# Polysketch attention and cosine router on one core: a reordered start of the early experts, key sums taken earlier, a routing maximum and a row write cut in two

## The chip, the cores and the metric

One Trainium2 chip, one core of it. The metric is the device time of one execution in microseconds (us), lower is better. The kernel before was run three times: 200.28, 197.08 and 200.38 us, a median of 200.28 us.

## The reference, cut to what matters

The first half is attention with a product feature map, without a softmax. `S1` and `S2` are 8 x 32, heads have 32 columns, so each key and query becomes 64 features. The second half takes the four heads' outputs as 128-column tokens, sends each of the 4352 tokens to one of eight experts by a cosine, and applies that expert's two-layer MLP.

```python
def phi(x):
    a = np.einsum('rd,bhsd->bhsr', S1, x)
    b = np.einsum('rd,bhsd->bhsr', S2, x)
    return np.einsum('bhsi,bhsj->bhsij', a, b).reshape(*x.shape[:-1], r * r)
q_p, k_p = phi(q), phi(k)                        # batch 4, heads 4, seq 1088
kv = np.einsum('bhsf,bhsd->bhfd', k_p, v)
z = np.sum(k_p, axis=2)
num = np.einsum('bhsf,bhfd->bhsd', q_p, kv)
den = np.einsum('bhsf,bhf->bhs', q_p, z)[..., None] + 1e-06
x = (num / den).transpose(0, 2, 1, 3).reshape(B * S, H * D)
...
logits = xn @ en.T / tau                         # xn, en: rows of x and expert_emb, normalised
expert_idx = np.argmax(logits, axis=1)
gate_w = softmax(logits)[token, expert_idx]
for e in range(E):                               # w1[e]: 128 x 1024, w2[e]: 1024 x 128
    h = np.maximum(x[mask] @ w1[e], 0.0)
    out[mask] = gate_w[mask, None] * (h @ w2[e])
```

## The kernel before, in words

**Stages.** Two batches are worked together as a half, m = 0 and m = 1; a half has 17 tiles of 128 tokens, held as 4 + 4 + 4 + 4 tiles and one rest tile ("r"). For each group of four, keys and queries are turned by TensorE (`ktr`, `qtr`), multiplied by the sketches (`kab`, `qab`, or `pairs` for the queries of half 0), and the two factors are multiplied into features (`kp`, `qp`, `prod`). The keys' features times the values are summed into one PSUM bank (`kv`), together with the factors' own sums; `total` copies that bank, `kve` turns it by head with two kinds of matmuls (`by_head`, and `ones_e` for the denominators) and `kz` copies the result. The queries' features, turned (`trqp`, `qpT`), times that matrix give attention outputs and expert logits at once (`nd`, 32 recorded matmul passes of about 1.3 us for a group), and VectorE divides (`x`, lines 672 to 684).

**Routing.** For half 0, once all four `x 0 ...` are there, `best` takes the maximum of each token's eight logits and subtracts it (lines 733 to 735), `pick` makes the one-hot choice, `write` sends the rows (128 columns of output and 8 logits) to HBM by `rows<-xg`, and a chain of VectorE and TensorE steps (`place 0`, `count`, `take`, `split`, `mark`, `find`, `sums`, `tokens`) gives the token numbers of the first blocks, `dst_i`, and the experts of these blocks. GpSimd then gathers rows (`fetch`, line 1043, tile `xs`), SyncE's queue loads the expert's first layer (`weights`, tile `wb`, 512 KB), and TensorE runs the blocks.

**The blocks.** 35 blocks of 128 tokens. Block i is `turn(i)` (one transpose), `up(i)` (16 recorded passes `ps_big<-xTb,wb`), a Relu on ScalarE (`hT`, line 1108), and `down(i)` (16 passes on `w_sb,hT` into the banks acc or ab). `down` chooses its expert at run time, so it needs all sixteen pieces of the second layers (`w_sb`, 256 KB each) on the chip.

**What sets the order.** The order on every engine is written by hand: `HEAD` and `ORDER` (lines 395 to 410) are lists of step names that are executed as they stand, `AFTER_TURN` adds the steps that stand behind `turn 1`. So half 1's `nd 1 0` and `nd 1 1` stand in front of `up(0)`, `nd 1 2` and `nd 1 3` between `turn 1` and `up(1)`. The step `ld` issues the next piece of half 1's values and queries and then of the second layers; each waits for the last TensorE instruction in front of it, and all loads, the row writes and the first layers share SyncE's one queue. `nd` and `up` take turns on the two double banks `ps_big`: `up(0)` reuses the bank of `nd 1 0` (free when `x 1 0` has read it), `nd 1 2` reuses that of `nd 1 1` (free when `x 1 1` has read it).

## Time and profile before

| | us |
|---|---|
| median of three runs (lowest, highest) | 200.28 (197.08, 200.38) |
| profiled execution, its own time | 199.14 |
| its span, first to last instruction | 197.2 |
| outside the span | 1.94 |
| TensorE matmuls busy in the span | 188.3 (95%) |
| TensorE weight loads busy | 177.8 (90%) |
| VectorE, ScalarE, GpSimd busy | 87.9, 99.1, 107.6 |
| granted TensorE clock | 1.00 throughout |

In the timeline a row is: start in us, duration, engine, line, operation, the tile written and the tiles read, shapes, count; the square bracket tells how long the engine had been idle before it and what ended that. A count of x16 on matmuls counts recorded passes; a 32-bit product of one pair of tiles shows as two. PEld is TensorE's loading of weights, which runs beside its matmuls. In a windows row stand the stretch, its length, the busy time of each engine, the granted clock, the share of the DMA engines' time and GB/s.

### The profile page before, as it was taken

The numbers are of one execution on the slowest core, as the hardware profiler recorded it, in microseconds if no ns is written. First come the engines' busy times: TensorE is split into PE (matmuls) and PEld (weight loads), VectorE is DVE, ScalarE is ACT, GpSimd is POOL, SyncE is SP. The second block draws the span as 40 slices with busy tenths as digits, with TensorE's granted clock in tenths as the row PEclk, the third lists the DMA queues.
The fourth block names the chain that finished last, engine by engine and source line by source line (L and its number), as shares of the span: only waits on it lengthen the run. The fifth ranks groups of instructions, "written<-read, shape, count | busy, mean of one in ns | idle before, by whom it ended". The sixth has DMA issues, their size and how long they took to land.

```text
span 197.2 us, 7104 instructions
## 1 busy us (share of the span) xinstructions
PE 188.3 (95%) x2667; PEld 177.8 (90%) x2667; DVE 87.9 (45%) x393; ACT 99.1 (50%) x280; POOL 107.6 (55%) x135
## 2 busy tenths in 40 slices
PE   7999899999979999999999999999999999999990
PEld 7677799788869999999999999999999999998890
DVE  6589868798378489922221221221221221222100
ACT  2675542437253456433564654654654654766430
POOL 4300054707713866565977767767767767733052
PEclk9999999999999999999999999999999999999999
DMA  5979968974799997544587686596665655540001
GB/s 139 345 203 276 237 172 221 331 232 124 201 281 330 285 338 209 188 136 149 149 263 237 158 288 201 155 281 211 161 195 182 160 200 180 150 137 12 3 20 32
DMA packets 29924, 38.32 MB, mean 194 GB/s; under 512 B 5721, under 2 KB 23394, under 8 KB 29890
## 3 DMA queue, kind: packets, MB, share of 16 engines
q1 hardware_dynamic: 27600, 33.18, 56.3%
q0 software_dynamic: 2240, 4.67, 7.6%
q8 instruction: 23, 0.38, 0.8%
q14 instruction: 11, 0.09, 0.2%
q10 hardware_dynamic: 50, 0.01, 0.0%
HBM read 33.25 MB, written 4.66 MB: 192 GB/s over the span
## 4 chain that ended last, share of the span: by engine, by line
PE 75%; DMA 12%; DVE 6%; issue 2%; ACT 2%; POOLq 1%; POOL 0%
PE ps_big L155 35%; PE ps_acc L155 14%; PE ps_ab L155 14%; DMA xs<-rows,dst_i 12%; PE ps_t L158 6%; PE ps_t L155 3%; PE ps_acc L111 1%; DVE xg L679 1%; DVE row L779 1%; PE ps_ab L158 1%; PE ps_acc L158 1%; POOLq L1300 1%; DVE qp L458 1%; PE ps_big L158 1%; ACT hT L1108 1%
## 5 line engine op out<-in xcount | busy, mean ns | idle before, releaser
L155 PE MATMUL ps_big<-xTb,wb 128*128 128x128 f32 (+2 forms) x608 | 70.6, 266 | 0.1
L155 PEld LDWEIGHTS ps_big<-xTb,wb 128*128 128x128 f32 (+1 forms) x608 | 66.7, 183 | 1.5 <-issue 0.9
L1149 POOL DMA_INDIRECT out_dram<-y,dst_i x35 | 36.4, 1041 | 42.3 <-ACT sq L1113 21.4
L1108 ACT ACTIVATE hT<-ps_big 128x1024 f32<-128x1024 f32 x35 | 35.8, 1023 | 41.3 <-issue 23.6
L1043 POOL DMA_INDIRECT xs<-rows,dst_i x35 | 36.7, 1048 | 13.0 <-issue 6.1
L155 PE MATMUL ps_acc<-w_sb,hT 128*128 (+2 forms) x288 | 35.1, 275 | 0.0
L1051 DVE COPY xTb<-ps_t 128x128 f32<-128x128 f32 x28 | 8.1, 291 | 57.3 <-issue 39.7
L155 PEld LDWEIGHTS ps_acc<-w_sb,hT 128*128 128x128 f32 (+2 forms) x288 | 33.3, 184 | 0.3 <-issue 0.2
L155 PE MATMUL ps_ab<-w_sb,hT 128*128 (+1 forms) x272 | 33.2, 275 | 0.0
L155 PEld LDWEIGHTS ps_ab<-w_sb,hT 128*128 128x128 f32 (+1 forms) x272 | 31.6, 187 | 0.1
L1114 POOL TENSOR_TENSOR norm<-norm,half_c 128x1 f32<-128x1 f32 x35 | 20.7, 595 | 5.2 <-ACT sq L1113 4.9
L1127 DVE TENSOR_SCALAR gate<-gate 128x1 f32<-128x1 f32 x35 | 5.3, 150 | 21.2 <-ACT probs L1124 19.7
L458 POOL TENSOR_TENSOR kp<-both 128x1024 f32<-128x1024 f32 (+1 forms) x4 | 7.2, 1812 | 12.5 <-ACT both L499 11.1
L155 PE MATMUL ps_big<-kz,held 128*64 128x82 f32 x256 | 10.7, 236 | 1.1 <-ACT xTb L1051 1.1
L1146 ACT ACTIVATE y<-ps_ab,gate 128x128 f32<-128x128 f32 x17 | 6.2, 367 | 10.9 <-PE ps_ab L155 7.1
L155 PEld LDWEIGHTS ps_big<-kz,held 128*64 128x64 f32 x256 | 9.5, 136 | 2.3 <-ACT hT L1108 1.3
L1113 ACT ACTIVATE sq<-xs 128x128 f32<-128x128 f32 x35 | 10.6, 302 | 1.5 <-DMA xs<-rows,dst_i 1.3
L1124 ACT ACTIVATE probs<-xs,norm 128x8 f32<-128x8 f32 x35 | 10.3, 295 | 1.3 <-DVE norm L1118 1.3
L1146 ACT ACTIVATE y<-ps_acc,gate 128x128 f32<-128x128 f32 x17 | 6.2, 366 | 9.4 <-PE ps_acc L155 7.0
L158 PE MATMUL ps_t<-ident,xs 128*128 128x128 f32 x35 | 9.8, 279 | 0.0
L425 ACT COPY qT<-ps_t 128x512 f32<-128x512 f32 (+1 forms) x10 | 5.1, 535 | 7.2 <-PE ps_t L158 7.2
L458 DVE TENSOR_TENSOR kp<-both 128x1024 f32<-128x1024 f32 (+1 forms) x6 | 6.4, 1088 | 2.9 <-ACT both L499 2.8
(254 smaller groups left out, 254.4 us busy)
## 6 DMA issues: line engine op xcount, KB each, us to landing
wb<-in_moe_w_dram SPq DMA_DIRECT2D x35, 512.0 KB
w_sb<-in_moe_w_dram SPq DMA_DIRECT2D x16, 256.0 KB
rows<-xg SPq DMA_DIRECT2D x4, 544.0 KB
q<-in_q_dram SPq DMA_DIRECT2D x6, 256.0 KB
k<-in_k_dram SPq DMA_DIRECT2D x3, 512.0 KB
held<-in_moe_w_dram SPq DMA_DIRECT2D x3, 512.0 KB
v<-in_v_dram SPq DMA_DIRECT2D x2, 512.0 KB
v<-in_v_dram SPq DMA_DIRECT2D x4, 256.0 KB
```

Of the source, the lines that this page charges most:

```text
L155: last["pe"] = nc.tensor.matmul(*args, **how)
L158: last["pe"] = nc.tensor.transpose(*args)
L458: last[tag] = engine.tensor_mul(t.rearrange("p j h (i k) -> p (j h) i k", i=R), ab[:, :, 0].unsqueeze(3).broadcast_to([P, n * H, R, R]), b ...
L1043: nc.gpsimd.indirect_dma_start(out=xs[i][:], out_offset=None, in_=rows[:2 * S if t == 0 else N + 1], in_offset=bass.IndirectOffsetOnAxis(a ...
L1051: (nc.scalar.copy if i < 2 or 4 <= i <= 8 else nc.vector.tensor_copy)(xT[i], ps[:, :P])
L1108: nc.scalar.activation(hT[i], ps, ACT.Relu)
L1113: nc.scalar.activation(sq, xs[i][:, :DM], ACT.Square, accum_out=norms[i])
L1114: nc.gpsimd.tensor_tensor(out=norms[i], in0=norms[i], in1=half_c, op=ALU.pow)
L1124: nc.scalar.activation(p, xs[i][:, DM:], ACT.Exp, scale=norms.pop(i)[:, 0:1], accum_out=gate[i])
L1127: nc.vector.tensor_scalar_add(gate[i], gate[i], PROB_EPS)
L1146: nc.scalar.activation(y, ps, ACT.Copy, scale=gate.pop(i)[:, 0:1])
L1149: d = nc.gpsimd.indirect_dma_start(out=out[:, :], out_offset=bass.IndirectOffsetOnAxis(ap=dst_i[t][:, j:j + 1], axis=0), in_=y[:], in_offs ...
```

## The change

Six edits, all in order or in how a step is cut:

1. The rest tiles' loads of half 0 are issued as keys, keys, queries, queries; their two value loads now follow half 1's two big key loads on SyncE's queue.
2. `kv0 1` stands directly after `kv0 0`, and `kv0 2` where `kv0 1` stood.
3. Some `ld` steps stand at other places; the order of the pieces is the same.
4. `best` is cut: tiles 0 to 7 (`best 0a`) after `x 0 1`, the other nine after `x 0 3`. The write of the first eight tiles' rows (`write 0a`) stands after `nd 0 2`; two of the second-layer pieces stand between it and the second write.
5. `kve` is cut into the four `by_head` matmuls (`kve a`), now ahead of `trqp 1`, and the eight `ones_e` ones (`kve b`) where all stood.
6. In front of `up(0)` TensorE runs `nd 1 0`, `nd 1 1`, `turn 0`, `trqp 2`, where it ran `nd 1 0`, `trqp 2`, `turn 0`, `nd 1 1`.

```diff
-            for i in range(2):
-                for which in "kvq":
+            for which in "kq":
+                for i in range(2):
                     load_rest(0, i, which)
         else:
             for i in range(2):
                 load(k_sb, k, m, i)
+            for i in range(2):
+                load_rest(0, i, "v")
...
-place emb; kp0 2; iotas; qtr0 3; clear 0; kv0 0; ld; pairs 2; sec 2 0; sec 2 1; prod 2 0; prod 2 1; kab0 3; ld; kb0 3; kp0 3; ktr0 r; qtr0 r;
-kv0 1; ld; kab0 r; kb0 r; pairs 3; ld; qab0 r; sec 3 0; sec 3 1; qb0 r; kp0 r; prod 3 0; prod 3 1; qp0 r;
-clear 1; ktr 0; ld; ld; kv0 2; kv0 3; ld; kv0 r
+place emb; kp0 2; iotas; qtr0 3; clear 0; kv0 0; ld; kv0 1; pairs 2; ld; sec 2 0; sec 2 1; prod 2 0; prod 2 1; kab0 3; ld; kb0 3; kp0 3; ktr0 r; qtr0 r;
+kv0 2; ld; kab0 r; kb0 r; pairs 3; ld; ld; qab0 r; sec 3 0; sec 3 1; qb0 r; kp0 r; prod 3 0; prod 3 1; qp0 r;
+clear 1; ktr 0; kv0 3; ld; kv0 r
...
-total0; lanes; shifts; digits; ktr 1; ld; ktr 3; kab 0 ab; kve0; ld; kz0; kb 0; kab 1 acc; ld; kp 0; kb 1; ktr 2; ld;
-nd 0 0; ld; ld; kab 3 ab; ld; x 0 0; ktr r; nd 0 1; ld; kab 2 t; kab r ab; ld; x 0 1; kb 2; trqp0r; nd 0 2; ld; kb 3; kp 1; kb r; nd 0 3; ld; x 0 2;
-kv 0; ld; kp 2; x 0 3; qtr 1; kp 3; qtr 0; ld; kv 2; qab 0 t; qb 0; kp r; best 0; kv 3; qtr 3; qtr r; qp 0;
-place 0; count; take 0; qtr 2; ld; kv 1; ld; kv r; trqp 0; total; split 0; qab 1 t; qab 3 ab; rest; mark 00; qb 1;
-qab r ab; mark 01; find; exp0; qab 2 acc; sums; qb 2; qpT 0; qb 3; qb r; qp 1; tokens; z1; trqp 1; qp 3; kve; fetch0; fetch 1;
-trqp 3; qpT 1; kz; qp 2; nd 1 0; ld; ld; qp r; others; w 1; x 1 0; qpT 3; norm 0; trqp 2; ld; turn 0; ld; nd 1 1; ld; x 1 1;
+total0; lanes; shifts; digits; ktr 1; ld; ktr 3; kab 0 ab; kve0; ld; kz0; kb 0; kab 1 acc; ld; kp 0; kb 1; ktr 2; ld; ld;
+nd 0 0; ld; kab 3 ab; ld; x 0 0; ktr r; nd 0 1; ld; kab 2 t; ld; kab r ab; ld; x 0 1; best 0a; kb 2; trqp0r; ld; nd 0 2; write 0a; ld; kb 3; kp 1; kb r; nd 0 3; ld; x 0 2;
+kv 0; kp 2; x 0 3; qtr 1; kp 3; qtr 0; kv 2; qab 0 t; qb 0; kp r; best 0; kv 3; qtr 3; qtr r; qp 0;
+place 0; count; take 0; qtr 2; kv 1; ld; kv r; ld; trqp 0; total; split 0; qab 1 t; qab 3 ab; rest; mark 00; qb 1;
+qab r ab; mark 01; find; exp0; qab 2 acc; sums; qb 2; qpT 0; qb 3; qb r; qp 1; tokens; z1; kve a; trqp 1; qp 3; kve b; fetch0; fetch 1;
+trqp 3; qpT 1; kz; qp 2; nd 1 0; ld; ld; qp r; others; w 1; nd 1 1; ld; x 1 0; qpT 3; norm 0; turn 0; ld; trqp 2; ld; x 1 1;
 qpT 2
...
-            if stage == 0:
+            if stage == "a":
                 s["kve"] = ps_small()[:, :4 * COLS].rearrange("p (i a n) -> p i a n", i=2, a=2)
...
+                return
+            if stage == "b":
                 for i in range(2):
                     for p in range(2):
...
-        def best():
-            mx = work.tile([P, n], F32, tag=f"mx_{n}", name="mx")
-            nc.vector.reduce_max(out=mx, in_=lg[g][:, :n], axis=AX.X)
-            nc.vector.tensor_sub(xg[g][:, :n, DM:DM + E], lg[g][:, :n], mx.unsqueeze(2).broadcast_to([P, n, E]))
+        def best(a=0, b=n):
+            mx = work.tile([P, n], F32, tag=f"mx_{n}", name="mx")[:, :b - a]
+            nc.vector.reduce_max(out=mx, in_=lg[g][:, a:b], axis=AX.X)
+            nc.vector.tensor_sub(xg[g][:, a:b, DM:DM + E], lg[g][:, a:b], mx.unsqueeze(2).broadcast_to([P, b - a, E]))
```

How the rows moved, at the three places that the prediction speaks of. In a row of the order stand the line, the operation, the tile written and the tiles read, the shape and the count of calls (a call shows as two passes in the profile).

TensorE ahead of the first block, before (`by_head,kv` and `ones_e,z` are `kve`; `ident,qp` into ps_big, into acc and ab, and again into acc and ab are `trqp 1`, `trqp 3` and `trqp 2`; `ident,xs` are `turn 0` and `turn 1`; `kz,held` are `nd 1 0`, `nd 1 1` and, last, `nd 1 2`):

```order
L158 MATMUL ps_big<-ident,qp 128x128 x8
L155 MATMUL ps_t<-by_head,kv 64x2x40 x4
L155 MATMUL ps_t<-ones_e,z 64x1 x8
L158 MATMUL ps_acc<-ident,qp 128x128 x4
L158 MATMUL ps_ab<-ident,qp 128x128 x4
L155 MATMUL ps_big<-kz_204,held 64x82 x16
L158 MATMUL ps_acc<-ident,qp 128x128 x4
L158 MATMUL ps_ab<-ident,qp 128x128 x4
L158 MATMUL ps_t<-ident,xs 128x128
L155 MATMUL ps_big<-kz_204,held 64x82 x16
L1055 TENSOR_LOAD exp_210
L155 MATMUL ps_big<-xTb,wb 128x128 x8
```

The same place on TensorE in the changed kernel:

```order
L155 MATMUL ps_t<-by_head,kv 64x2x40 x4
L158 MATMUL ps_big<-ident,qp 128x128 x8
L155 MATMUL ps_t<-ones_e,z 64x1 x8
L158 MATMUL ps_acc<-ident,qp 128x128 x4
L158 MATMUL ps_ab<-ident,qp 128x128 x4
L155 MATMUL ps_big<-kz_204,held 64x82 x32
L158 MATMUL ps_t<-ident,xs 128x128
L158 MATMUL ps_acc<-ident,qp 128x128 x4
L158 MATMUL ps_ab<-ident,qp 128x128 x4
L1061 TENSOR_LOAD exp_210
L155 MATMUL ps_big<-xTb,wb 128x128 x8
```

The `by_head` matmuls moved ahead of `trqp 1`; `nd 1 1` moved up to `nd 1 0` (x32 together), and what stands directly ahead of `up(0)` is now `trqp 2`. ScalarE's and GpSimd's own orders are the same as before.

VectorE after `x 0 1` of half 0, in the changed kernel (the rows on `ps_big` and `parts` are `x`):

```order
L689 TENSOR_REDUCE lg<-parts 128x32
L740 TENSOR_REDUCE mx<-lg 128x8
L741 TENSOR_TENSOR xg<-lg,mx 128x8x8
L682 TENSOR_SCALAR rc<-ps_big 128x16
L683 RECIPROCAL rc<-rc 128x16
L684 TENSOR_TENSOR xg<-ps_big,rc 128x4x128
```

Before, `x 0 2` (the three rows from `rc<-ps_big` on) followed directly on `x 0 1`, and the two rows of `best` stood once, after `x 0 3`, with 17 tiles; now they stand there with the last nine.

SyncE's queue around the row writes, in the changed kernel (`w_sb` are `ld` steps on the second layers):

```order
L208 DMA w_sb<-in_moe_w_dram 128x4x128 x6
L791 DMA rows<-xg 128x1088
L208 DMA w_sb<-in_moe_w_dram 128x4x128 x2
L791 DMA rows<-xg 128x1088
L795 DMA rows<-xg 64x136 x2
L208 DMA w_sb<-in_moe_w_dram 128x4x128 x2
L1061 TENSOR_LOAD exp_210
```

Before, all eight `w_sb` pieces stood ahead of both big row writes. What follows on this queue (the first layer of block 0, two pieces, that of block 1, four pieces, those of blocks 2 and 3) has the same order in both.

16 lines of the change are left out of this document (9 added, 7 removed).

## The prediction

> **What bounds the kernel now.** I read the page first, then windows over the stages, then TensorE's timeline, and looked up who ended each of its waits.
>
> ```profile
> span 197.2 us, 7104 instructions
> PE 188.3 (95%) x2667; PEld 177.8 (90%) x2667; DVE 87.9 (45%) x393; ACT 99.1 (50%) x280; POOL 107.6 (55%) x135
> ```
>
> ```profile
> 10.00:22.00 12.00, 12.00 (x352) 9.19 (x349) 10.65 (x27) 7.97 (x21) 0.55 (x4) 1.00 0.91 250
> 22.00:31.00 9.00, 8.16 (x184) 7.17 (x184) 6.80 (x20) 4.02 (x12) 3.03 (x2) 1.00 0.71 186
> 31.00:46.00 15.00, 14.25 (x384) 12.62 (x380) 12.86 (x41) 5.40 (x14) 6.70 (x5) 1.00 0.82 241
> 46.00:60.00 14.00, 12.79 (x208) 11.15 (x207) 8.99 (x26) 7.15 (x21) 7.98 (x9) 1.00 0.77 217
> 90.00:110.00 20.00, 20.00 (x180) 20.00 (x180) 5.20 (x33) 11.33 (x35) 15.14 (x18) 1.00 0.68 204
> ```
>
> TensorE (PE) is the bound. In the stretch of the blocks, the last row, it stands still for nothing (20.00 of 20.00 us, weight loads too), and the change touches no block's own matmuls. All edits lie ahead of that, so they can only pay with the time that TensorE stands still in the head: 0, 0.84, 0.75 and 1.21 us in the four rows above, 2.8 of 199. That is less than 2%, about what a measurement of this kernel can tell from no change. The question is which of these gaps the edits reach.
>
> ```profile
> 24.34 0.37 PE L155 MATMUL ps_t<-by_head,kv 128*64 128x80 f32 x5 [0.83 <-issue]
> 45.09 1.09 PE L158 MATMUL ps_big<-ident,qp 128*128 128x128 f32 x8 [0.27 <-DVE qp L458]
> 46.11 0.50 PE L155 MATMUL ps_t<-by_head,kv 128*64 128x80 f32 x8
> 46.98 0.66 PE L158 MATMUL ps_acc<-ident,qp 128*128 128x128 f32 x4
> 48.01 1.36 PE L155 MATMUL ps_big<-kz,held 128*64 128x82 f32 x32
> 49.30 0.65 PE L158 MATMUL ps_acc<-ident,qp 128*128 128x128 f32 x4
> 50.23 0.27 PE L158 MATMUL ps_t<-ident,xs 128*128 128x128 f32 x1
> 50.43 1.36 PE L155 MATMUL ps_big<-kz,held 128*64 128x82 f32 x32
> 51.78 2.63 PE L155 MATMUL ps_big<-xTb,wb 128*128 128x128 f32 x16
> 55.63 1.36 PE L155 MATMUL ps_big<-kz,held 128*64 128x82 f32 x32 [1.10 <-ACT xTb L1051]
> 62.65 1.96 PE L155 MATMUL ps_big<-xTb,wb 128*128 128x128 f32 x16
> ```
>
> The largest gap, 1.10 us, stands in front of `nd 1 2` (55.63). The row names ScalarE's copy, but `nd 1 2` needs the bank of `nd 1 1`, which VectorE frees:
>
> ```profile
> 50.52 0.28 DVE L683 TENSOR_TENSOR parts<-ps_big,rc 128x128 f32<-128x128 f32 x1
> 50.83 0.38 DVE L684 TENSOR_REDUCE lg<-parts 128x32 f32<-128x128 f32 x1
> 54.10 0.18 DVE L677 TENSOR_SCALAR rc<-ps_big 128x16 f32<-128x16 f32 x1 [2.88 <-remote]
> 55.20 0.28 DVE L683 TENSOR_TENSOR parts<-ps_big,rc 128x128 f32<-128x128 f32 x1
> ```
>
> `x 1 1` reads the bank until 55.48, and `nd 1 2` starts 0.15 us later. VectorE had been idle since 51.21; it began 2.3 us after the recorded end of `nd 1 1` (50.43 + 1.36 = 51.79), released by something that the profile doesn't name ("remote").
>
> **The change part by part.** The sum is made on the profiled execution, 199.14 us: its span of 197.2 and 1.94 around it.
>
> *`nd 1 1` ahead of `turn 0` and `trqp 2`.* TensorE's work is the same. `trqp 2` (49.30 to 50.23) and `turn 0` (to 50.43) move behind `nd 1 1`, which ends 1.13 us earlier, at 50.66. `x 1 1` can follow `x 1 0` at 51.2. Even if VectorE is again 2.3 us late, it starts at 53.0 and has read the bank 1.38 us later (54.10 to 55.48 before), at 54.3; TensorE, behind `turn 1`, is free at 55.63 - 1.10 = 54.53. The gap closes: **-1.10**, with bounds of -1.10 and the loss of the last rival. `trqp 2`'s copies on ScalarE come about 1.3 us later; they feed `nd 1 2`, 2 us on, and `up(0)` covers them. `turn 0` starts 0.2 us later than where it found its gathered rows without a wait. `up(0)` starts no later: `x 1 0` has read its bank at 50.80.
>
> *`kve a` ahead of `trqp 1`.* The gap of 0.27 at 45.09 gets the `by_head` matmuls, 0.5 us at most. They read ScalarE's copy of the sums, which was ready at 41. But `trqp 3` (46.98) waits for VectorE's second `qp`:
>
> ```profile
> 40.67 0.32 ACT L528 COPY kv<-ps_acc 128x192 f32<-128x192 f32 x1
> 45.72 1.21 DVE L458 TENSOR_TENSOR qp<-ps_ab,qb 128x1024 f32<-128x1024 f32 x1
> ```
>
> It ends at 46.93, so TensorE only trades its wait for one at `trqp 3`, unless VectorE's chain gets shorter too. So this pays only what the next edit frees.
>
> *`best` in two.* Before:
>
> ```profile
> 31.89 0.17 DVE L677 TENSOR_SCALAR rc<-ps_big 128x16 f32<-128x16 f32 x1 [0.44 <-PE ps_big L155]
> 35.69 0.30 DVE L734 TENSOR_REDUCE mx<-lg 128x17 f32<-128x136 f32 x1
> 36.02 0.70 DVE L735 TENSOR_TENSOR xg<-lg,mx 128x136 f32<-128x136 f32 x1
> 39.13 0.17 DVE L880 TENSOR_SCALAR full<-ps_big 128x8 f32<-128x8 f32 x1 [0.98 <-PE ps_big L155]
> 61.65 0.22 DVE L735 TENSOR_TENSOR xg<-lg,mx 128x64 f32<-128x64 f32 x1
> ```
>
> The subtraction for eight tiles takes 0.22 (61.65), their maximum no more than that for 17, 0.30: 0.5 for the pair, and it falls into the idle 0.44 ahead of `x 0 2`: +0.06. The nine-tile pair, 0.5 as well, replaces 1.03 (35.69 to 36.72): -0.5. But VectorE then waits 0.98 for the placing matmuls, and TensorE's own work stands ahead of these; most of the 0.5 only makes that wait longer. With the edit above **-0.15** (bounds 0 and the whole gap, -0.27).
>
> *Key sums, rest loads, `ld`, the first row write.* TensorE has no gap from 10 to 22, so moving `kv` there frees **0**; what covers the moved sums is that their features come from VectorE a stage ahead, and if these were late the first row would fall under 12.00. The row writes go out at 36.75 and the gathers that read them at 45.42, so the earlier write is hidden by the routing chain: **0**. The rest tiles' value loads now stand behind half 1's keys, which go out until 15.1; the sums that need them start at 21.14: **0**, and each microsecond beyond these 6.0 would stop TensorE.
>
> ```profile
> 13.23 1.86 SPq L140 DMA_DIRECT2D k<-in_k_dram  x2
> 21.14 0.41 PE L155 MATMUL ps_acc<-kp,v_rest 128*32 128x64 f32 x16
> 36.75 0.97 SPq L785 DMA_DIRECT2D rows<-xg  x2
> 45.42 1.45 POOL L1043 DMA_INDIRECT xs<-rows,dst_i  x1 [5.61 <-DVE dst_i L872]
> 57.90 1.21 SPq L1060 DMA_DIRECT2D wb<-in_moe_w_dram  x2
> ```
>
> *What is late next.* So far TensorE saves 1.25 us. Then it comes to `up(2)` at 62.65, whose first layer is issued only at 57.90, behind the piece of second layers that waits for `nd 1 2`.
>
> ```profile
> 51.00:57.00 6.00, 4.79 (x73) 4.00 (x69) 2.13 (x8) 2.31 (x5) 2.34 (x3) 1.00 1.04 298
> 57.00:60.00 3.00, 3.00 (x52) 2.74 (x53) 2.64 (x8) 1.76 (x9) 1.56 (x3) 1.00 0.82 202
> 60.00:64.00 4.00, 4.00 (x38) 4.00 (x37) 3.45 (x19) 1.78 (x6) 1.04 (x2) 1.00 0.96 363
> ```
>
> The DMA engines are full from 51 to 57, slack from 57 to 60 (0.82), full again to 64. An earlier `nd 1 2` lets the layer be issued earlier, but the queue can give back only its slack, (1.00 - 0.82) x 3 = 0.54, and the 0.15 by which the burst begins earlier: 0.7. If the layer landed just as `up(2)` took it, the gain is cut from 1.25 to 0.7; if it landed half a microsecond ahead, it is not cut. I take **+0.40**, towards the late end, because the next block's layer is issued right behind it and shares the engines.
>
> Sum: -1.10 - 0.15 + 0.40 = -0.85. 199.14 - 0.85 = **198.3 us**. The profiled execution lies 0.6% under the median of the runs shown (200.28) and next to their mean (199.25), so the number stays on its base; on the median's it would be 199.4.
>
> **The rivals.**
>
> *The loads give nothing back.* The layer of `up(2)` lands at 62.6 in both, since the queue's order is fixed and it is full. For it: 1.04 and 0.96 on either side. Against: 0.82 between. Only 0.15 remains: 199.0.
>
> *The unnamed stall goes, or comes again.* TensorE stood 0.83 us in the midst of `by_head` (24.34), waiting for nothing that the profile shows; the same matmuls at 46.11 had no such gap. The edits change what the DMA engines carry around it. If it goes, 199.14 - 0.85 - 0.83 = 197.5. If it comes at two more places, +1.66: 200.0. The program's code is itself loaded during the run:
>
> ```profile
> q8 instruction: 23, 0.38, 0.8%
> ```
>
> That is 16.5 KB a packet, beside the data. The Trainium skill (Runtime: NRT & Kernel Launch, Instruction fetch mechanics) holds that such block fetches are mostly hidden in straight code; by it the stall would not be a fetch, its chance would fall, and 198.3 would stand. No row here names the stall's cause.
>
> *Slower: the lateness belongs to `nd 1 1` itself.* If the 2.3 us between its recorded end and its reader are TensorE's own, they move ahead with it, and `turn 0`, `trqp 2` and `up(0)` queue behind: 50.66 + 2.28, then 1.13 for the two, 1.79 for `up(0)` (sixteen passes, as in the chain's row below) and 0.2 for `turn 1`: 56.06 for `nd 1 2` against 55.63. It turns into a loss when the lateness is over 1.85 us. With 0.15 gained ahead of it: 199.14 + 0.43 - 0.15 = 199.4.
>
> ```profile
> 54.45 1.02 ACT L1108 ACTIVATE hT<-ps_big 128x1024 f32<-128x1024 f32 x1 [2.32 <-PE ps_big L155]
> 61.03 1.79 PE ps_acc L155 x16
> ```
>
> Against it: ScalarE took `up(0)`'s result at 54.45, and 1.79 us of passes don't fit between 54.1 and that. The Trainium skill (Perfetto Trace Analysis, Summary: the profiler window per engine type) calls TensorE's reported end an estimate, which by itself would speak for this rival and 199.4.
>
> **How the numbers follow.** Forecast 198.3: 0.42. Loads give nothing, 199.0: 0.18. Stall gone, 197.5: 0.17; stalls more, 200.0: 0.10. Lateness moves, 199.4: 0.13. All lie within 2% of the time before, since the head holds only 2.8 us; the rest is the spread of the runs, 197.08 to 200.38. The range takes 197.5 less 1.1 and 200.0 plus 0.6 of that spread: 196.4 to 200.6. Faster by over 2%: 0.07, from the stall's case in a low run; slower by over 2%: 0.05, from the cases above 199.14 in a high one; within 2%: 0.88.
>
> **What would show it.** Right: `nd 1 2` without a gap, starting near 54.4; `x 1 1` starting before 53; no gap at `trqp 1`; VectorE's wait at `full` near 1.4; `up(2)` near 61.8, with a short wait for a load there or shortly ahead; a DMA share from 57 to 60 near 1. Wrong: a gap over 0.3 us in front of `turn 0` or of the rest tile's key sums, `up(2)` still at 62.6, or a time outside 196.4 to 200.6.

## The result, and the profile after

The changed kernel took **199.82 us** in the median of six runs (199.36 to 201.71) beside 198.32 for the kernel before (six runs, 197.08 to 200.38). The ratio is **1.0119 [1.0079, 1.0158]**: slower by 1.2%, where 0.85 us less had been forecast. Two later timings of the same program gave 1.0050 [1.0006, 1.0093] and 1.0052 [1.0000, 1.0103]. Ratios leave out runs more than 1.5% above a kernel's fastest; the medians that stand beside them are over all runs. So the change costs between a half and 1.2 per cent. The profiled execution of the changed kernel took 199.99 us, with a span of 198.0 (before 199.14 and 197.2).

The page of the changed kernel, its first lines:

```profile
span 198.0 us, 7108 instructions
PE 187.6 (95%) x2667; PEld 177.2 (89%) x2667; DVE 89.0 (45%) x395; ACT 99.1 (50%) x280; POOL 107.7 (54%) x135
```

TensorE is as busy as before (187.6 against 188.3 us). The span is 0.8 longer, so TensorE stood still for longer. The windows of the changed kernel show where:

```profile
10.00:22.00 12.00, 11.20 (x335) 8.27 (x335) 9.90 (x26) 7.46 (x20) 0.72 (x5) 1.00 0.89 244
22.00:31.00 9.00, 8.71 (x208) 7.48 (x199) 7.34 (x22) 4.21 (x12) 2.71 (x1) 1.00 0.76 204
31.00:46.00 15.00, 13.42 (x384) 12.06 (x384) 12.43 (x40) 5.43 (x15) 6.44 (x4) 1.00 0.79 241
46.00:60.00 14.00, 13.14 (x217) 11.95 (x217) 11.02 (x32) 7.52 (x24) 9.15 (x10) 1.00 0.73 210
57.00:60.00 3.00, 2.34 (x44) 2.21 (x40) 2.71 (x8) 1.39 (x9) 2.15 (x4) 1.00 1.17 319
60.00:64.00 4.00, 3.12 (x26) 2.75 (x25) 2.98 (x18) 1.71 (x5) 0.45 (x1) 1.00 1.03 383
```

TensorE's idle time in the first four stretches is 0.80, 0.29, 1.58 and 0.86 us, where it had been 0, 0.84, 0.75 and 1.21. From 60 to 64 it is 0.88 where it had been 0. The DMA engines, slack from 57 to 60 before (0.82), are now full there. TensorE's timeline names the places; the bracket is the idle time ahead of a row and what ended it:

```profile
19.37 0.22 PE L155 MATMUL ps_t<-Sblk,kT 128*64 128x64 f32 x1 [0.79 <-issue]
24.70 0.42 PE L155 MATMUL ps_t<-by_head,kv 128*64 128x80 f32 x5 [0.29 <-issue]
38.36 0.22 PE L155 MATMUL ps_big<-oh,before 128*128 128x136 bf16 x1 [0.26 <-DVE oh L750]
40.10 0.32 PE L155 MATMUL ps_big<-oh,ones 128*128 128x56 bf16 x7 [1.02 <-issue]
48.38 0.66 PE L158 MATMUL ps_acc<-ident,qp 128*128 128x128 f32 x4 [0.20 <-DVE qp L460]
49.40 2.50 PE L155 MATMUL ps_big<-kz,held 128*64 128x82 f32 x64
52.87 1.95 PE L155 MATMUL ps_big<-xTb,wb 128*128 128x128 f32 x16
54.86 1.37 PE L155 MATMUL ps_big<-kz,held 128*64 128x82 f32 x32
58.83 2.02 PE L155 MATMUL ps_big<-xTb,wb 128*128 128x128 f32 x16 [0.66 <-DVE rc L683]
61.65 2.02 PE L155 MATMUL ps_acc<-w_sb,hT 128*128 x16 [0.69 <-DMA w_sb<-in_moe_w_dram]
63.86 2.02 PE L155 MATMUL ps_big<-xTb,wb 128*128 128x128 f32 x16 [0.19 <-DVE gate L1134]
```

Set against the rows of before, the delay of the changed kernel runs like this. `nd 0 0` starts at 26.64, before at 26.23: **+0.41**; a new stop of 0.79 ahead of it, and 0.54 less in the old one in `by_head`. At `nd 1 0` it is 49.40 against 48.01: **+1.39**; a wait of 0.26 and a stop of 1.02 (0.21 before) in the placing matmuls. At `nd 1 2` it is 54.86 against 55.63: **-0.77**; the gap of 1.10 is gone, and `up(0)` runs through in 1.95 where it had taken 2.63. At `up(2)` it is 63.86 against 62.65: **+1.21**; `up(1)`, `down(0)` and `up(2)` now wait 0.66, 0.69 and 0.19. So the gain at `nd 1 2` was real, 2.16 us, and all but 0.18 of it was given back at once; what remains is the loss of the head.

### The profile page after: what moved, and what is told of

The parts are those of the page before. It is cut to its first block, busy times and chain, and to the rows that moved or that the text cites. A ratio compares the mean times of both kernels' runs of the same rounds, so it can differ in the third digit from the quotient of the medians.

```text
span 198.0 us, 7108 instructions
## 1 busy us (share of the span) xinstructions
PE 187.6 (95%) x2667; PEld 177.2 (89%) x2667; DVE 89.0 (45%) x395; ACT 99.1 (50%) x280; POOL 107.7 (54%) x135
## 4 chain that ended last, share of the span: by engine, by line
PE 72%; DMA 12%; DVE 9%; issue 3%; ACT 1%; POOLq 1%; POOL 0%
PE ps_big L155 33%; PE ps_ab L155 15%; PE ps_acc L155 13%; DMA xs<-rows,dst_i 12%; PE ps_t L158 6%; PE ps_t L155 2%; PE ps_acc L111 1%; DVE qp L460 1%; DVE xg L684 1%; DVE xg L741 1%; DVE row L785 1%; PE ps_ab L158 1%; DVE lg L689 1%; POOLq L1306 1%; DVE rc L683 1%
## 5 line engine op out<-in xcount | busy, mean ns | idle before, releaser
L155 PE MATMUL ps_big<-xTb,wb 128*128 128x128 f32 (+2 forms) x608 | 69.8, 266 | 0.8 <-DVE rc L683 0.7
```

What stands on the lines that cost most here:

```text
L155: last["pe"] = nc.tensor.matmul(*args, **how)
```

## The experiments

Four theories run through the expectations, by these letters or in words. **F**, instruction fetch: the stops marked "issue" are TensorE waiting for its own next instructions, whose packets queue behind data. **V**, VectorE: the early subtraction waits for GpSimd and so delays `x 0 2` and all of the routing. **L**, loads: time gained ahead of the blocks is given back by transfers that land when they did before. **S**, the stop: the lateness of the readers of `nd 1 1` and `turn 0` belongs to TensorE's order and moves along with it. In the diffs of the order, the piece of the row that changes is shown.

### One edit at a time

Each group of edits was put alone into the kernel before, and one was taken out of the changed kernel. The query group alone (e1):

```diff
-... w 1; x 1 0; qpT 3; norm 0; trqp 2; ld; turn 0; ld; nd 1 1; ld; x 1 1;
+... w 1; nd 1 1; ld; x 1 0; qpT 3; norm 0; turn 0; ld; trqp 2; ld; x 1 1;
```

> The kernel before with one edit alone: nd 1 1 ahead of x 1 0, turn 0 and trqp 2. Theory (loads give it back): nd 1 2 starts without a gap about 1.2 us earlier than in before (near 54.4), but up 1 then waits up to 0.7 for VectorE, down 0 or up 2 waits for its load, and up 2 starts within 0.5 of 62.65; the time is within 0.3% of before (ratio 0.997 to 1.003). Rival (the gap closed is time gained): up 2 starts 1 us earlier, ratio near 0.994. Second rival (the move itself is what made the changed kernel slower): up 2 later than 63.2, ratio 1.005 or more.

The changed kernel with the head of before (e2), that is, without the spread key sums and with the first loads in their old order; its diff against the changed kernel is the change's own diff of `HEAD` and of the first loads, backwards:

```diff
-            for which in "kq":
-                for i in range(2):
+            for i in range(2):
+                for which in "kvq":
...
-                load_rest(0, i, "v")
```

> The changed kernel with the head of before: key sums, order of the first loads and loads in the head as in before; the split maximum, the early write, the by_head matmuls and nd 1 1 stay as changed. Theory (TensorE waits for its own next 256 instructions when data fills the DMA engines, at its instructions 705, 961 and 1729): no stall over 0.3 at instruction 705 (19.4 in the changed kernel), the one at 961 back near 0.8; what stays is the part at 32 to 41 us; the time lies between before and the changed kernel, ratio 1.003 to 1.010. Rival (the loss comes from the query group and the loads behind it): as slow as the changed kernel, 1.010 to 1.014.

The split maximum and row write alone (e3):

```diff
-... ld; x 0 1; kb 2; trqp0r; nd 0 2; ld; kb 3; ...
+... ld; x 0 1; best 0a; kb 2; trqp0r; nd 0 2; write 0a; ld; kb 3; ...
```

> The kernel before with the maximum in two parts and the first tiles' rows written early, nothing else. Theory (the early subtraction runs beside GpSimd's third product and takes 1.0 instead of 0.2): VectorE's subtraction near 31.7 takes 0.9 to 1.1, x 0 2 starts about 0.8 later than in before, TensorE's placing matmuls wait up to 0.3 for VectorE; ratio 1.001 to 1.005. Rival (the split is harmless or gains): subtraction 0.2, ratio 0.997 to 1.000.

The head alone (e4): before, with the change's `HEAD` and first loads, that is, e2's diff the other way round.

> The kernel before with the changed head alone: key sums spread, order of the first loads, loads in the head. Theory (instruction fetch): a new stall of 0.5 to 1.0 at TensorE's instruction 705 (about 19.4), the one at 961 smaller than 0.83, nd 0 0 starts 0.2 to 0.8 later than 26.23; ratio 1.001 to 1.004. Rival (head edits cost nothing, as predicted): no stall there, ratio 0.998 to 1.001.

The changed kernel once more, beside the next experiments (c1) and beside the last ones (k3), with no edit:

> The changed kernel itself, timed again beside the variants. If its loss is a property of the program: ratio 1.008 to 1.016 again, with stalls that no engine's row names at TensorE's records 705, 961 or 1729. If its loss was an accident of the runs it was first timed in: ratio under 1.005.

> The changed kernel, beside the two others on the same chip: ratio to before 1.005 to 1.015, stall at record 1729 of 1.0 to 1.6, idle time at up 0 in some runs, that is a clock under 0.993 in some 4 to 8 of 12.

The changed kernel without the split (g1), so with one `best` and one `write`:

```diff
-... x 0 1; best 0a; kb 2; trqp0r; ld; nd 0 2; write 0a; ld; kb 3; ...
+... x 0 1; kb 2; trqp0r; ld; nd 0 2; ld; kb 3; ...
```

> The changed kernel without the split maximum and without the early write: one pair over seventeen tiles, rows written after it. Theory (VectorE's early subtraction beside GpSimd's product makes the placing late): TensorE's wait for oh at the placing (0.26) goes, x 0 2 starts without the extra microsecond; if the early write of 0.5 MB also delays the packet for record 1729, the stall there shrinks from 1.02 to under 0.5; the time 0.3 to 1.3 under the changed kernel's. Rival (the loss lies in the head's key sums and the query group): no faster than the changed kernel.

Measured, with the medians over all runs and those of the kernel before in the same comparison:

| kernel | ratio, 95% | median, before |
|---|---|---|
| e1 query group alone | 1.0011 [0.9967, 1.0054] | 199.97, 199.19 |
| e2 changed, head of before | 1.0139 [1.0077, 1.0201] | 202.25, 199.19 |
| e3 split alone | 1.0005 [0.9968, 1.0041] | 199.57, 199.19 |
| e4 head alone | 0.9983 [0.9951, 1.0015] | 198.68, 199.19 |
| c1 changed | 1.0050 [1.0006, 1.0093] | 201.59, 199.38 |
| k3 changed | 1.0052 [1.0000, 1.0103] | 201.57, 199.19 |
| g1 changed, no split | 1.0005 [0.9969, 1.0042] | 199.58, 199.38 |

No edit alone makes a difference that these runs show; `kve a` was not run alone. The head does not carry the loss: without it (e2) the loss is there, and no smaller. Between e1 and e2, whose intervals lie apart, stand the split, `kve a` and the places of the `ld` steps; and without the split (g1) no loss is seen. This points to the split, in company, since alone (e3) no loss is seen either. It does not show it: the intervals of g1 and c1 overlap.

Several of these expectations missed. e2's ratio came where its rival had put it. e3's slow subtraction came as told, but its ratio lies just under its range, and k3's stop at record 1729 was 0.59 for the 1.0 to 1.6 expected. c1's ratio lies between its two cases. e4's stop at record 705 was 0.24 for the 0.5 to 1.0 expected, and its ratio too was the rival's. e1's ratio was the expected one, but not for the reason given: nothing waits for a load at `up(1)`, `down(0)` or `up(2)` in its profile; a stop of 1.91 in front of `up(0)` took the gain (see "The start of the blocks").

### What the split costs on VectorE

The changed kernel's VectorE, the two subtractions and the first routing step that waits for the placing matmuls:

```profile
32.14 0.98 DVE L741 TENSOR_TENSOR xg<-lg,mx 128x64 f32<-128x64 f32 x1
37.08 0.23 DVE L741 TENSOR_TENSOR xg<-lg,mx 128x72 f32<-128x72 f32 x1
40.52 0.17 DVE L886 TENSOR_SCALAR full<-ps_big 128x8 f32<-128x8 f32 x1 [1.78 <-PE ps_big L155]
```

GpSimd's row in the same execution:

```profile
31.09 1.96 POOL L460 TENSOR_TENSOR kp<-both 128x1024 f32<-128x1024 f32 x1 [1.34 <-ACT both L501]
```

The subtraction over eight tiles took 0.98 us, the one over nine tiles 0.23. The long one lies beside GpSimd's product, which ends at 31.09 + 1.96 = 33.05; it ends at 33.12. `x 0 2` starts at 33.05 where it had started at 31.89, 0.75 later than the 0.41 that everything was late there. The kernel before has the same thing in one piece: its subtraction over all seventeen tiles (36.02, 0.70 long) began while GpSimd's products ran until 36.57:

```profile
34.03 2.54 POOL L458 TENSOR_TENSOR kp<-both 128x1024 f32<-128x1024 f32 x2 [1.39 <-issue]
```

To tell this from chance, h2 puts `best 0a` and `write 0a` behind `x 0 2`:

```diff
-... x 0 1; best 0a; kb 2; trqp0r; ld; nd 0 2; write 0a; ld; kb 3; kp 1; kb r; nd 0 3; ld; x 0 2;
+... x 0 1; kb 2; trqp0r; ld; nd 0 2; ld; kb 3; kp 1; kb r; nd 0 3; ld; x 0 2; best 0a; write 0a;
```

> The changed kernel with the first eight tiles' maximum behind x 0 2 instead of ahead of it, and their rows written where before wrote them. Theory (the subtraction is slow where GpSimd's third product runs beside it): the subtraction over 128 x 64 takes 0.2 to 0.3 instead of 0.98, x 0 2 starts as in the kernel without the split, no wait for oh at the placing; 0.2 to 0.4 us under the kernel with the late write alone. Rival (the subtraction is slow wherever it stands): 0.9 to 1.0 again.

VectorE of h2, the same subtraction:

```profile
33.80 0.23 DVE L741 TENSOR_TENSOR xg<-lg,mx 128x64 f32<-128x64 f32 x1
```

GpSimd of h2:

```profile
30.63 1.96 POOL L460 TENSOR_TENSOR kp<-both 128x1024 f32<-128x1024 f32 x1 [1.34 <-ACT both L501]
```

The product has ended at 32.59, and the subtraction takes 0.23. TensorE's wait for `oh` in front of the placing matmuls, 0.26 to 0.28 us in all ten profiled executions with `best 0a` ahead of `x 0 2`, is gone in h2, k1 and g1. V is shown in the traces: `x 0 2` starts 0.75 us late, and TensorE waits 0.26 to 0.28. VectorE won most of the 0.75 back, since the nine-tile pair took 0.49 (36.82 to 37.31) where the pair over seventeen had taken 1.03; the placing matmuls start 0.18 later than the 0.41. The Trainium skill (SBUF — State Buffer, Summary: rules for kernel authors) says that a VectorE operation with two SBUF inputs, while GpSimd reads SBUF, makes the second of the two to issue wait until the first has finished; the trace agrees, 0.98 beside the product against 0.23 behind it. In time h2 came to 1.0016 [0.9971, 1.0060], with a median over all runs of 201.29 beside 198.96: eight of its twelve runs had a mean granted clock under 0.993, of which more below. So V's own share is not read from the time.

### The stops that wait for nothing

F says that the stop follows TensorE's instruction count. f1 adds 32 matmuls to the warm-up (64 records), whose result nothing uses:

```diff
+    for _ in range(32):
+        nc.tensor.matmul(ps_warm[:2 * R, :2 * R], zeros[:, :2 * R], zeros[:, :2 * R], start=True, stop=True)
     keep_warm(6)
```

> The kernel before with 32 more warm-up matmuls at the start, that is 64 more TensorE instructions ahead of everything else (the result is not used by anything). Theory (TensorE waits for its next block of 256 instructions): the unnamed stalls stay at records 193 + 256 k of TensorE (705, 961, 1729, 1985), which are now other matmuls: none in front of the fifth by_head matmul any more, but 32 matmuls ahead of it. Rival (the stall belongs to the work that stands there): a stall in front of the by_head matmul again, now record 1025, and at the ones matmul of the placing, now record 1793.

TensorE of f1, its stops marked "issue" up to 42 us:

```profile
19.14 0.36 PE L157 MATMUL ps_acc<-kp,v 128*32 128x64 f32 x10 [0.79 <-issue]
23.14 0.32 PE L157 MATMUL ps_acc<-kp,v 128*32 128x64 f32 x8 [0.38 <-issue]
41.54 0.31 PE L157 MATMUL ps_acc<-kp,v_rest 128*32 128x64 f32 x5 [0.39 <-issue]
```

f1 was run once, in 201.30 us. The stop in `by_head` is gone from there, and the stops stand in front of other work, 64 records earlier in the program. Counting TensorE's records in order of start (matmuls, weight loads and its sequencer's own), they are the records 705, 961 and 1985 in f1 as in all other kernels: 193 + 256 k. A group of matmuls is cut in two there; nothing in the kernel has this step. The other side of it is the queue q8, 23 packets of 16 KB, one for each 256 records. In the changed kernel's DMA view from 37.4 to 38.6 us:

```profile
q1 hardware_dynamic: 647, 0.39, 105.9%
q8 instruction: 1, 0.02, 5.3%
```

From 33.9 to 37.4 there is none. The packet is on its way from 37.46 to 38.48, the DMA engines are full (105.9%), and TensorE stands still until 40.10. The twenty profiles hold 42 stops of this kind of over 0.15 us, and in all of them TensorE went on 1.2 to 1.7 us after its packet's end. The packet for record 1729, worked out from the trace's packets and TensorE's records: how long after TensorE had entered the block before (record 1473) it went out, and the stop at 1729.

| kernel | packet goes out after, us | stop, us |
|---|---|---|
| before | 2.62 | 0.21 |
| changed; c1; k3 | 3.37; 4.05; 3.29 | 1.02; 1.43; 0.59 |
| e1, e3, g1, f1 | 2.08, 2.57, 1.84, 0.33 | 0 |
| h1, h4, j3 | 2.03, 1.90, 1.62 | 0 |
| e2, e4, f2 | 4.01, 3.89, 3.79 | 1.38, 1.58, 1.42 |
| h2, h3, j4 | 4.53, 3.87, 3.69 | 2.15, 1.37, 1.14 |
| j2, k1, k2 (loads behind) | 1.40, 1.12, 1.09 | 0 |

The block lasts about 4.8 us (33.69 to 38.52 in the kernel before). A packet that goes out within 2.6 us of its beginning is in time or nearly so, one that goes out after more than 3.2 is not. In the late ones it went out after the first big row write had been issued; so it did in four that are in time (e3, h1, j2, k1), and in the other early ones it went ahead of it. What delays it, the row write or the pieces of the second layers, was asked with three kernels. f2 moves `ld` steps back to where they stood before:

```diff
-... kp 0; kb 1; ktr 2; ld; ld;
-nd 0 0; ld; kab 3 ab; ...
+... kp 0; kb 1; ktr 2; ld;
+nd 0 0; ld; ld; kab 3 ab; ...
...
-kv 0; kp 2; x 0 3; qtr 1; kp 3; qtr 0; kv 2; ...
+kv 0; ld; kp 2; x 0 3; qtr 1; kp 3; qtr 0; ld; kv 2; ...
```

> The changed kernel with the loads that are spread over the query groups and the placing (not those of the head) back at their places in before. Theory (data moved to 30 to 36 us delays the packet of TensorE's next instructions): the packet for record 1729 starts under 3.0 us after the block before it was entered (3.37 in the changed kernel), the stall there is under 0.5 (1.02), the time 0.5 to 1.2 under the changed kernel's, ratio to before 1.002 to 1.008. Rival (the stall does not hang on these loads): stall about 1, same time as the changed kernel.

h1 leaves `best 0a` where it is and moves its write:

```diff
-... nd 0 2; write 0a; ld; kb 3; ...
-... kp r; best 0; kv 3; ...
+... nd 0 2; ld; kb 3; ...
+... kp r; write 0a; best 0; kv 3; ...
```

> The changed kernel with the first eight tiles' rows written where before wrote them; the maximum stays split. Theory (the early write of half a megabyte stands ahead of TensorE's instruction packet): the packet for record 1729 starts under 3.0 us after record 1473 was entered (3.4 to 4.0 where the write is early), the stall there is under 0.5, the time 0.6 to 1.5 under the changed kernel's: ratio 0.999 to 1.005. Rival (the split maximum alone makes the placing late): stall as before near 0.2, but VectorE's row still 1.0 and the wait for oh 0.27, ratio at most 0.3% under the changed kernel's.

j2 moves five pieces of the second layers behind `best 0`:

```diff
-... x 0 1; best 0a; kb 2; trqp0r; ld; nd 0 2; write 0a; ld; kb 3; kp 1; kb r; nd 0 3; ld; x 0 2;
-... best 0; kv 3; qtr 3; qtr r; qp 0;
+... x 0 1; best 0a; kb 2; trqp0r; nd 0 2; write 0a; kb 3; kp 1; kb r; nd 0 3; x 0 2;
+... best 0; ld; ld; kv 3; ld; qtr 3; qtr r; ld; qp 0;
```

> The changed kernel with five of the eight second-layer pieces that go out from 28 to 36 us moved behind the rows' write (which stays early). Theory (data queued ahead delays TensorE's instruction packet): the packet for record 1729 starts under 2.0 us after record 1473 was entered, against 3.4 to 4.5 in the changed kernel, no unnamed stall over 0.3 there, and the time falls by 0.8 to 1.4 us against the changed kernel: ratio 1.000 to 1.007. Rival (the packet's lateness does not come from the data): it starts 3.4 or more after again, with a stall of 1.0 or more.

k2 does the same with the kernel before:

> The kernel before with five second-layer pieces behind the rows' write, else unchanged. Theory (what the loads' place costs is the instruction packet, and that is on time in before already): stall at record 1729 0 instead of 0.2, ratio 0.996 to 1.000. Rival (the loads' place gains by itself in any kernel): ratio 0.990 to 0.995.

f2 missed: five of its pieces went out 1.1 to 2.5 us later than in the changed kernel, counted from the entry of the block, but all still ahead of the packet, which was as late as ever (3.79, with a stop of 1.42 where under 0.5 had been expected); the ratio was 1.0028 [0.9989, 1.0068]. h1 had no stop there, and 1.0040 [1.0005, 1.0074]; but h2, which issues on SyncE in the same order, had 2.15, and e4, without any early write, 1.58. The early write is therefore not the cause by itself; small shifts decide on which side of it the packet falls. No single edit is shown to make this stop either: e4 has it with the changed head alone, and e2 without it. j2 is clear. Its DMA engines in the window ahead of the placing matmuls, with the share in the last column but one:

```profile
34.00:37.00 3.00, 2.92 (x106) 2.53 (x105) 2.76 (x10) 1.45 (x3) 2.19 (x2) 1.00 0.20 78
```

and TensorE of j2:

```profile
37.60 0.22 PE L155 MATMUL ps_big<-oh,before 128*128 128x136 bf16 x1 [0.28 <-DVE oh L750]
37.78 0.70 PE L155 MATMUL ps_big<-oh,ones 128*128 128x128 bf16 x16
51.37 1.96 PE L155 MATMUL ps_big<-xTb,wb 128*128 128x128 f32 x16
53.37 1.36 PE L155 MATMUL ps_big<-kz,held 128*64 128x82 f32 x32
```

The engines are at 0.20 where the kernel before had 0.98 and c1 0.91 in the same window, the packet goes out 1.40 us after the block before was entered, and the sixteen placing matmuls run in one piece, while V's wait of 0.28 stays. So F is shown for this place. That the pieces of the second layers are what the packet stood behind rests on three kernels: with five of them out of its way (j2, k1, k2) it goes out after 1.09 to 1.40 us, and there is no stop; in the seventeen others it goes out after 1.62 us or more (f1 aside, whose count is shifted), and ten of them stop. Of the 60 crossings at records 705, 961 and 1729 in the twenty profiles 36 have a stop, of up to 2.15 us; all the others together have 6. The Trainium skill (Runtime: NRT & Kernel Launch, Instruction fetch mechanics) gives blocks of 256 instructions and 16 KiB, and these rows agree. The same section of the Trainium skill says that crossing from one to the next is mostly hidden; at these three records it is not. The prediction drew on it.

In time, j2 was 1.0039 [0.9999, 1.0080] and k2 0.9975 [0.9937, 1.0013]. Both include 1. The stop was removed, and no shorter kernel is shown for it; why not stays open.

At record 705 all twelve kernels with the new head have a stop (0.18 to 1.44), with the old head at most 0.27 (f1 aside, whose records are shifted); there 961 in `by_head` had most of it (0.50 to 1.22 but in e1, 0). Added up, 705 and 961 cost 1.0 us on the mean with the new head and 0.7 with the old: the head moves this stop more than it makes one. The traces show how. The block before record 705 lasts 3.64 us in the changed kernel and 5.08 in the kernel before; the one before record 961 lasts 5.04 and 3.40. The packets go out at much the same time after the entry, 1.82 and 1.86 us in the changed kernel, 1.73 and 1.71 before. In the short block that makes a stop of 0.79 and 0.83, in the long one of 0.29 and of nothing.

### The start of the blocks

One of the prediction's rivals was that the lateness moves along with `nd 1 1`. TensorE of c1:

```profile
40.25 0.32 PE L155 MATMUL ps_big<-oh,ones 128*128 128x56 bf16 x7 [1.43 <-issue]
51.97 0.33 PE L158 MATMUL ps_t<-ident,xs 128*128 128x128 f32 x1
55.07 2.55 PE L155 MATMUL ps_big<-xTb,wb 128*128 128x128 f32 x16 [1.89 <-issue]
```

ScalarE of c1, the copy that `up(0)` needs:

```profile
54.75 0.27 ACT L1057 COPY xTb<-ps_t 128x128 f32<-128x128 f32 x1 [3.76 <-remote]
```

`turn 0` (51.97) has ended at 52.30 by its record, ScalarE copies its result 2.45 us later, and `up(0)` starts after 1.89 us of standing still. In the first profile of the changed kernel, of the same program, the copy came at once and `up(0)` did not wait. The cost goes on; two windows of c1, the clock in the column behind the engines:

```profile
56.00:58.00 2.00, 2.00 (x16) 1.67 (x16) 0.71 (x4) 0.88 (x3) 0.00 (x0) 0.61 0.89 257
58.00:60.00 2.00, 2.00 (x32) 1.94 (x30) 0.00 (x0) 0.84 (x2) 0.00 (x0) 0.53 0.91 255
```

In the trace the granted clock is 0.50 from 56.45 to 59.86, 3.4 us. Four kernels go at this. h3 is the changed kernel with the query-group row of before, that is, e1's diff backwards:

> The changed kernel with nd 1 1 back behind trqp 2 and turn 0. Theory (two costs: the late instruction packet at the placing, and TensorE standing for turn 0 behind nd 1 1 long enough that its clock is halved): the stall at record 1729 stays at 1.0 to 1.5, but the mean granted clock is over 0.993 in at least 10 of 12 runs (7 of 12 in the changed kernel), and the time is 0.3 to 1.0 under the changed kernel's. Rival (the order of nd 1 1 gains what it closes): 0.5 to 1.1 over the changed kernel's.

h4 is e1 with `turn 0` in front of `nd 1 1`:

```diff
-... w 1; nd 1 1; ld; x 1 0; qpT 3; norm 0; turn 0; ld; trqp 2; ld; x 1 1;
+... w 1; turn 0; ld; nd 1 1; ld; x 1 0; qpT 3; norm 0; trqp 2; ld; x 1 1;
```

> The kernel before with nd 1 1 moved ahead of trqp 2 alone: turn 0, nd 1 1, x 1 0, trqp 2. Theory (what costs is turn 0 behind nd 1 1, since up 0 waits for its copy): no idle time over 1 us in front of up 0, no stretch at half clock, mean clock over 0.993 in at least 10 of 12 runs, nd 1 2 without a gap over 0.5, ratio 0.993 to 0.999. Rival (what TensorE gains here the loads take back): ratio 0.999 to 1.003 with the clock as said.

j3 is h4 with five `ld` steps of the query-group row put into the placing row, where the queue has room:

```diff
-... kv 1; ld; kv r; trqp 0; total; split 0; qab 1 t; qab 3 ab; rest; mark 00; qb 1;
+... kv 1; ld; kv r; ld; trqp 0; total; ld; split 0; qab 1 t; ld; qab 3 ab; rest; mark 00; qb 1; ld;
...
-... nd 1 0; ld; ld; qp r; others; w 1; turn 0; ld; nd 1 1; ld; x 1 0; ...
+... nd 1 0; qp r; others; w 1; turn 0; nd 1 1; x 1 0; ...
```

> The kernel with turn 0 and nd 1 1 ahead of trqp 2 (else as before), and five second-layer pieces issued between 41 and 47 us instead of 48 to 56. Theory (the loads take back what the query group gains): up 1 no longer waits 1.0 for its first layer nor down 0 for its second; up 2 starts before 62.0 where the head is not late, ratio 0.992 to 0.998. Rival (the gain is lost elsewhere): up 1 and down 0 wait for another engine, ratio 0.998 to 1.003.

j4 is the changed kernel with the second gather behind `turn 0`, since GpSimd's gathers run while TensorE stops:

```diff
-... trqp 1; qp 3; kve b; fetch0; fetch 1;
+... trqp 1; qp 3; kve b; fetch0;
...
-... turn 0; ld; trqp 2; ld; x 1 1;
+... turn 0; fetch 1; ld; trqp 2; ld; x 1 1;
```

> The changed kernel with the gathers of rows 1 to 4 issued behind turn 0 instead of right behind the first gather. Theory (GpSimd's gathers hold up TensorE between the first query group and up 0): ScalarE copies turn 0's result within 0.3 us of the record's end, TensorE idles under 0.6 in front of up 0, mean clock over 0.993 in at least 10 of 12 runs, and turn 1 may wait up to 1 us for its rows. Rival (the gathers have nothing to do with it): the copy comes 1.5 to 3 us after the record's end again, idle time of 1.3 to 2.6 in front of up 0, clock under 0.993 in 5 or more of 12 runs.

The four came to 1.0077 [1.0039, 1.0114] (h3), 1.0011 [0.9977, 1.0045] (h4), 1.0116 [1.0068, 1.0164] (j3) and 1.0102 [1.0046, 1.0157] (j4). Three of them missed: h3 was to be faster than the changed kernel, with at most two of twelve runs under a clock of 0.993, and comes out higher, with four such runs; the ratios of h4 and j3 were to be under 1. So putting the order back does not by itself give the time back. How long the stretch takes that the edit was to shorten, from the start of `nd 1 0` to that of `up(2)` in each profiled execution, shows more:

| order | us from `nd 1 0` to `up(2)` |
|---|---|
| `nd 1 1` behind `turn 0` and `trqp 2` | before 14.64, e3 14.28, e4 14.88, h3 14.38, k2 14.93, f1 15.91 |
| `nd 1 1` ahead of both | j2 13.15, changed 14.46, k3 13.92, j4 14.32, f2 14.60, e1 16.25, h1 16.24, h2 16.24, c1 16.36, g1 16.68, e2 16.92, k1 16.97 |
| `turn 0`, `nd 1 1`, `trqp 2` | h4 15.85, j3 14.17 |

The old order is even, 14.3 to 14.9, but for f1, where `down(0)` waited 0.89 for a piece of the second layers. With the new one there is a stop in front of `up(0)` in nine of the twelve, 1.17 to 2.58 us. In the changed kernel's first profile and in j4 there is none, and the stretch is about as long as before. In j2 there is none either, and the stretch is the shortest of all. In k3 and f2 the clock stayed at 1.00 behind the stop (1.17 and 1.85), and the stretch is no longer than before; in the other seven the clock is halved behind it, and the stretch is about 2 us longer.

The halving lowers a run's mean granted clock to under 0.993. Such a mean is in 51 of all 126 runs of the twelve, in 7 of 48 with the old order in e3, e4, h3 and k2, and in 15 of 139 of the kernel before. But this stop is not the only one with a halved clock behind it. In h3 and e4, with the old order, it stands behind the stops of 1.37 and 1.58 at record 1729, and in g1 a second time behind the 1.44 at record 705. A window of e4:

```profile
40.00:44.00 4.00, 4.00 (x86) 3.43 (x86) 3.79 (x15) 0.90 (x2) 0.00 (x0) 0.57 0.63 178
```

So the counts of runs do not tell S from F. S is shown in the profiles: the edit turns a gap of 0.29 to 1.10 in front of `nd 1 2` into a stop in front of `up(0)` in nine of twelve of them, and in seven it costs more than the gap, by the clock. In the three timings of the changed kernel runs with the low mean were 0 of 6, 7 of 12 and 6 of 12, so the first, 1.0119, owes nothing to a halved clock.

What the stop is, stays **open**. It is not F: the packet for record 2241, the last such border ahead of `up(0)`, had ended over 4 us before TensorE came to that record in all nine. TensorE's load of the block's expert number (L1061), which stands in its order in front of `up(0)`, was not varied. The gathers were, in j4: it has no stop, and its copy comes 0.04 us after `turn 0`'s end, as it should if the gathers were the cause.

```profile
52.29 0.27 ACT L1057 COPY xTb<-ps_t 128x128 f32<-128x128 f32 x1 [1.38 <-PE ps_t L158]
```

But the changed kernel's first profile and j2 have no stop either, with the gathers in place, so one profile does not tell. And in j4 `turn 1` then waits for its rows:

```profile
56.53 0.33 PE L158 MATMUL ps_t<-ident,xs 128*128 128x128 f32 x1 [1.61 <-DMA xs<-rows,dst_i]
```

In some profiles the loads take the gained time back, as L says. In h4 TensorE waits 0.40 for a copy in front of `trqp 2` and 0.16 in front of `up(0)`, starts `nd 1 2` at 54.95 without a gap, and then:

```profile
59.26 2.02 PE L155 MATMUL ps_big<-xTb,wb 128*128 128x128 f32 x16 [1.00 <-DMA wb<-in_moe_w_dram]
61.77 2.02 PE L155 MATMUL ps_acc<-w_sb,hT 128*128 x16 [0.38 <-DMA w_sb<-in_moe_w_dram]
```

Here the first layer is named in front of `up(1)`, where the changed kernel's row named VectorE, which had read the bank by 57.66; that it was the layer there too is argued from this row. j3 moved the pieces out of that stretch, and the rows that the gathers fetch came later instead: `turn 0` waited 1.34 us for them. Its `up(1)` and `down(0)` wait for nothing, as expected, and `up(2)` starts at 61.48; why its ratio is 1.0116 all the same is not shown.

In j2 the loads take nothing back. Nothing waits at `up(1)`, `down(0)` and `up(2)`:

```profile
56.61 2.05 PE L155 MATMUL ps_big<-xTb,wb 128*128 128x128 f32 x16
58.76 2.02 PE L155 MATMUL ps_acc<-w_sb,hT 128*128 x16
60.78 2.02 PE L155 MATMUL ps_big<-xTb,wb 128*128 128x128 f32 x16
```

So the edit can gain what it was to gain, and more: 13.15 us where the kernel before took 14.64. Two things speak against counting on it. j2, j3 and j4 ran on a chip of their own, beside a kernel before of 197.44 in the median, where the other comparisons have 198.32 to 199.38, so part of the 1.5 may belong to that chip. And this profiled execution is the fastest of j2's twelve runs, which together are no faster than before.

### All known costs out

k1 is h2 with the load places of j2: no early subtraction, no late packet at 1729.

> The changed kernel with five second-layer pieces behind the rows' write, the first maximum behind x 0 2 and its rows written where before wrote them: the head's edits and nd 1 1 stay. Theory (these are the changed kernel's costs): no unnamed stall over 0.3 at record 1729, no wait for oh, no slow subtraction; ratio to before 0.994 to 1.001, and 1 to 2 us under the changed kernel run beside it. Rival (the order of nd 1 1 costs by itself): idle time over 1.3 in front of up 0 and a clock under 0.993 in 5 or more of 12 runs, ratio 1.002 or more.

It came to 1.0028 [0.9992, 1.0064], median 200.29 beside 199.19, with six of twelve runs under a clock of 0.993. Both costs, V and the stop at 1729, are out of its profile as they should be, but the time is what the rival had said: S, 2.12 us in front of `up(0)`, is left. No version is shown to beat the kernel before.

### All kernels side by side

With `best 0a` ahead of `x 0 2` the nine kernels e2, e3, f2, h1, h3, j2, j4, c1 and k3 have a mean ratio of 1.0059 (from 1.0005 to 1.0139); without it e1, e4, g1, h2, h4, k1 and k2 have 1.0004 (0.9975 to 1.0028). j3 (1.0116), which has no split, is left out, as its gathers were late; with it the second mean is 1.0018. This is the strongest sign in the times that the split is the part that costs, and no proof. The two groups differ in other edits as well, and most intervals overlap, so its share by V and its share by F are not told apart in time; each is shown in the profiles only.

## Why the prediction was wrong, point by point

**TensorE is the bound, and the head's gaps are all there is to win.** Right: it is as busy as before, and in the profiled execution every difference came from its standing still between 19 and 64 us.

**`nd 1 1` ahead, -1.10.** The gap closed as forecast, in the profiled execution even with more (-2.16 at `nd 1 2`). That `nd 1 2` then started at 54.86, near the 54.4 that was named, is partly luck: `nd 1 0` was 1.39 late, and the lateness of `x 1 1`, which had been reckoned with, did not come. In nine of the twelve profiles with this order the rival "the lateness belongs to `nd 1 1` itself" took its place. The step that failed there is "`up(0)` starts no later": it looked at the bank of `up(0)` alone, which also needs the copy of `turn 0`, and that came 1.7 to 3.2 us after `turn 0`'s end. The rival had 0.13 and a price of +0.43 at `nd 1 2`. The place was the right one, and the price was off both ways: next to nothing while the clock stayed up, about 2 us where it was halved.

**`kve a` and `best` in two, -0.15.** This step failed in its price. The traded gap came as told: none at `trqp 1`, 0.20 at `trqp 3`. But the eight-tile subtraction was costed at 0.22, from a row (61.65) beside which GpSimd did nothing; at its new place it took 0.98 behind GpSimd's product. The pair was to cost 0.06 on VectorE's path; it cost 0.75. The nine-tile pair paid as forecast, 0.49 for 1.03, so 0.18 was left, and TensorE waited 0.26 at the placing matmuls, which the prediction took to be covered. VectorE's wait at `full` grew to 1.78, for the 1.4 forecast.

**Key sums, loads, first row write, 0.** This is the step that failed most. It asked which instruction waits for these transfers, and nothing does. It did not ask what else goes through the same DMA engines: TensorE's own code. Stops marked "issue" rose by 0.25 in the head (+0.79, -0.54) and by 0.81 in the placing matmuls. The rival "the stall comes again at two more places" had this mechanism as a guess and, at 200.0, nearly the time (199.82 measured, 199.99 in the profile). That nearness is luck: it kept the gain of 0.85 and put 1.66 of stalls on top, and in the profile the stops added 1.06 and the gain was gone. It was given 0.10, partly because no row of the trace of before tied the stall to the packets. One could have: the records' numbers, 961 and 1729, both 193 + 256 k.

**The loads give back, +0.40.** Too small by far in the profiled execution. At `nd 1 2` 2.16 us were gained, at `up(2)` 0.18 were left. The rival "the loads give nothing back" had worked out 0.15 for this, and was right in size. Its mechanism is named by the row at `down(0)` (0.69 for a load) and argued at `up(1)` (0.66); j2, with the same order of loads from there on, kept its gain. Its time of 199.0 missed what was lost ahead of `nd 1 0`.

**The sum.** -1.10 - 0.15 + 0 + 0.40 was forecast. What came, in the same terms and in the profiled execution: -2.16 up to `nd 1 2`, +1.98 given back, +1.39 ahead of it, together +1.21 at `up(2)`; 0.4 of that came back within the blocks, and the span is 0.8 longer. The signs that would show it wrong were named, a gap over 0.3 ahead of the rest tile's key sums among them; the stop of 1.02 stood in the placing matmuls instead, just ahead of those sums.
